# Step order in a fused attention and expert kernel: where the turn, the mix, the row-sum reciprocal and the gate's chain stand in four in-order queues

## The chip, the cores and the metric

The kernel runs on one core of one Trainium2 chip. The metric is the device time of one execution in microseconds, as the median over several executions. Five engines work side by side: PE (TensorE, matmuls and transposes), DVE (VectorE), ACT (ScalarE), POOL (GpSimd) and SP, which only issues transfers. Each takes its own instructions in the order in which the program wrote them.

## The reference, cut to what matters

```python
scores = scale * np.matmul(q, k.transpose(0, 1, 3, 2))        # 4 x 8 heads, 576 x 576, head_dim 64
kth = np.partition(scores, -32, axis=-1)[..., -32:-31]
scores = np.where(scores >= kth, scores, -1e9)
attn = np.exp(scores - np.max(scores, axis=-1, keepdims=True))
attn = attn / (np.sum(attn, axis=-1, keepdims=True) + 1e-09)
x = np.matmul(attn, v)                                        # -> 2304 tokens x 512
...
x = (x @ w_a) * (x @ w_b) @ w_out                             # 512 -> 1536 -> 512, gated
...
expert_idx = np.argmax(logits, axis=1)                        # logits of a cosine router, 8 experts
out[mask] = gate_w[mask, None] * (np.maximum(x[mask] @ w1[e], 0) @ w2[e])
```

Three stages follow one another: attention that keeps the 32 largest scores of each row, a gated feed-forward layer, and a layer of eight experts of which each token takes one.

## The kernel before, in words

**Rows and parts.** The attention is cut into 144 rows of work. A row is 128 query rows of one head pair against 576 keys. Four or five rows, in some stretches one, that share a pair of heads make a part of N = 256, 320 or 64 tokens; there are 36 parts. The main loop (line 919) runs over steps; in step s several rows are in flight, each at another stage. `scores` (359) of row s+2 is two halves of matmuls on PE, each followed by a copy to the tile `s` on ACT (372). `topk` (375) of row s is seven long passes on DVE, spread over two steps. `softmax` (399) of row s-2 is a Relu on ACT (404), then a small product and a subtraction on POOL (406, 407), and one step later an Exp on ACT (409) that also leaves the row sum in `sm`. `turn` (411) of row s-4 transposes the result on PE in two halves (426), each copied out by ACT (429). The tile `s` has five buffers (`SB`), so that the first copy of row s+2 needs the subtraction of row s-3.

**A part's end.** When the last row j of a part has been turned, in step j+4, `mix` (457) is put on a list, and its matmuls with the values (467) run in step j+5, followed by `along` (439), which turns the inverted row sums `rc` along the tokens with small matmuls (447) and copies them to `xR` on ACT (455). `sums` (432) adds 1e-9 on POOL at the start of step j+4 (435) and takes the reciprocal on DVE at the start of step j+5 (437), ahead of the long passes of that step. `finish` (477) multiplies by `xR` on POOL (479), splits the product into two parts and stores them; its pieces are taken one at a time in slots 2 and 4 of the following steps by `piece` (905).

**Background.** The gated layer, `moe1` (646), works on nine groups of 256 tokens. A group can start when its tokens have been finished, two steps later. It is a generator that hands out a few matmuls at a time (727 for the two first products, 674 for the second). `run` (884) carries out one slot of a step and then lets `background` (848) issue gated work worth `share[0]`. The share is set once a step (lines 992 to 1001): the allowance `STEP` = 5.4 (4.5 before step 38), less 0.54 for a turn, 0.48 or 0.96 for scores, 0.44 for turns of queries and keys, and N/100 as long as a mix is on the list, divided by the number of slots. A mix stays on the list for two steps: in the first it runs, in the second `run` finds it finished and takes it off, and no background is called for that slot.

**The gate's chain.** For each block f of a group ACT copies both products to `gab` (741), POOL multiplies them, ACT makes `gh`, POOL makes `gl` (all through line 661, `tick`, from the list `pend`); a tick comes after each four matmuls, seven to a block, and takes one entry of the list. Before, a block puts four entries on it: product, nothing, `gh`, `gl`.

**Order.** The order on PE, DVE, ACT and POOL is that of the program text (`manual_schedule`, 878). An instruction that waits holds all that stand behind it on its engine. Steps from `S1` = 19 on are called late; about 117 us have passed by then. After the last row the rest of the gated layer runs, then the experts.

Of the kernel before, what the change touches and what calls it, by code (L numbers as in the profile page):

```python
# [37 lines left out]
F0 = 1  # L38
# [47 lines left out]
def fused_kernel(  # L86
# [26 lines left out]
    NP = H // 2  # L113
# [91 lines left out]
    with ExitStack() as ph:  # L205
# [251 lines left out]
        def mix(o):  # L457
            N = o.N
            while pieces:
                piece()  # L460
            o.xsb = wk.tile([P, 320], F32, name="xsb")
            o.xh = wk.tile([P, 320], F32R, name="xh", bufs=1)
            p = ps.tile([P, 512], F32, name="tr", bufs=NTR)
            for c in range(5):
                ks = slice(0, P) if c < 4 else slice(64, P)
                for h in range(2):
                    pe.matmul(  # L467
                        p[h * 64 : h * 64 + 64, :N], o.vs[ks, h, c], o.wt[h][ks, c, :N], start=(c == 0), stop=(c == 4)
                    )
            act.activation(o.xsb[:, :N], p[:, :N], AF.Copy)  # L470
            along(o)
            pieces.append(finish(o))
            yield N / 100

        xg0 = [mk.tile([P, KC, GN], F32R, name=f"xg{i}", bufs=XG) for i in range(2)]

# [169 lines left out]
        def moe1(G):  # L646

            gi = G.gi
            g0, N = GROUPS[gi]
            G.inputs()  # L650
            xg, ws = G.xg, G.ws
            LA = WB // 2 - 1
            while len(ws) < LA:
                G.load()
            px = [None, None]
            gs = {}
            pend = []

            def tick():
                if pend:  # L660
                    pend.pop(0)[1]()  # L661

            def second(f, tiles=(0, 1)):
                while pend and pend[0][0] <= f:
                    tick()
                hi, lo = gs[f]
                if gi == 0:
                    conv.need(2, f)
                for t in tiles:
                    ts = slice(t * P, (t + 1) * P)  # L670
                    if f == 0:
                        px[t] = mp.tile([P, DM], F32, name="x1", bufs=2)
                    for i, (g, w) in enumerate(((lo, 0), (hi, 1), (hi, 0))):
                        pe.matmul(  # L674
                            px[t], g[:, ts], wo[:, w, f], start=(f == 0 and i == 0), stop=(f == NF - 1 and i == 2)
                        )
                    if f == NF - 1:
                        r = route(g0 // P + t, px[t])
                        next(r)
                        routes.append(r)  # L680
                        debt[1] = 0.0
                    tick()
                    yield 0.64

            begun = {}
            if gi == 0:
                for f in range(2):
                    while not (conv.ready(0, f) and conv.ready(1, f)):
                        yield None
                    begun[f] = [mp.tile([P, 512], F32, name=nm, bufs=2)[:, :256] for nm in ("ab", "x1")]  # L690
                    for i in range(2):
                        wt = conv.tiles[i, f]
                        for c in range(KC - 1):
                            for a, x in TERMS1:
                                pe.matmul(
                                    begun[f][i],
                                    wt[:, a, c, :],
                                    xg[x][:, c, :],
                                    start=(c == 0 and (a, x) == TERMS1[0]),
                                    stop=False,  # L700
                                )
                            yield 3 * N / 2400
                while ready[0] < N:
                    yield None

            for f in range(NF):
                nxt = todo[1][1] if len(todo) > 1 and todo[1][0] <= now[0] else None
                if f >= (NF - 4 if gi else NF - 1) and nxt:
                    nxt.inputs()
                if f + LA < NF:  # L710
                    G.load()
                elif nxt:
                    nxt.load()
                if gi == 0:
                    conv.begun = f
                    while now[0] < NRW and not (conv.ready(0, f) and conv.ready(1, f)):
                        yield None
                    for i in range(2):
                        conv.need(i, f)
                    ws[f] = [conv.tiles[i, f] for i in range(2)]  # L720
                ab = mk.tile([P, 2, GN], F32, name="gab")
                p = None if f in begun else mp.tile([P, 2, 256], F32, name="ab", bufs=2)
                ps_ = begun[f] if f in begun else [p[:, 0], p[:, 1]]
                for i, wt in enumerate(ws[f]):
                    terms = [(a, x, c) for (a, x) in TERMS1 for c in range(KC) if f not in begun or c == KC - 1]
                    for j, (a, x, c) in enumerate(terms):
                        pe.matmul(  # L727
                            ps_[i],
                            wt[:, a, c, :],
                            xg[x][:, c, :],  # L730
                            start=(j == 0 and f not in begun),
                            stop=(j == len(terms) - 1),
                        )
                        if j % 4 == 3 and (i == 0 or j < 11):
                            tick()
                            yield 4 * N / 2400
                if f in begun:
                    for i in range(2):
                        act.activation(ab[:, i], ps_[i], AF.Copy)
                else:  # L740
                    act.activation(ab, p, AF.Copy)  # L741
                recent[0] = ab
                yield 4 * N / 2400
                hi = mk.tile([P, GN], F32R, name="gh", bufs=LAG + 2)
                lo = mk.tile([P, GN], F32R, name="gl", bufs=LAG + 2)
                gs[f] = hi, lo
                pend.append((f, partial(pool.tensor_tensor, ab[:, 0], ab[:, 0], ab[:, 1], op=OP.mult)))
                pend.append((f, lambda: None))
                pend.append((f, partial(act.activation, hi, ab[:, 0], AF.Copy)))
                pend.append((f, partial(pool.tensor_tensor, lo, ab[:, 0], hi.bitcast(F32), op=OP.subtract)))  # L750
                if f >= LAG:
                    yield from second(f - LAG)
            tail[0] = tail[0] if gi == len(GROUPS) - 1 else lambda: None
            nxt = todo[1] if len(todo) > 1 and todo[1][0] <= now[0] and todo[1][1].ws else None
            if nxt:
                nxt[2] = moe1(nxt[1])
            for tiles in ((0,), (1,)) if gi == len(GROUPS) - 1 else ((0, 1),):
                for f in range(NF - LAG, NF):
                    for _ in range(6 if nxt else 0):
                        yield next(nxt[2])  # L760
                    for _ in range(NTF if tiles[0] >= ET else 0):
                        tail[0]()
                    yield from second(f, tiles)
# [155 lines left out]
        for step in range(-AHEAD_L, NRW + TL + 5):  # L919
# [24 lines left out]
            with tc.high_priority(offset=FG):  # L944
# [2 lines left out]
                    next(soft, None)  # L947
                soft, old = softmax(live[step - 2]) if 0 <= step - 2 < NRW else none, soft
                j = step - 5
                if 0 <= j < NRW and rows[j][4] and made[rows[j][:3]].n >= F0 * NP:  # L950
                    sums(made[rows[j][:3]], False)
                j = step - 3 if step < S1 else step - 4 if step > S1 else -1
                summed = made[rows[j][:3]] if 0 <= j < NRW and rows[j][4] else None
                if summed:
# [3 lines left out]
                for n in range(4):  # L958
                    next(thresholds[0], None)
                    next(cur, None)  # L960
                    if n == 3 and summed and summed.n < F0 * NP:
                        sums(summed, False)
                if step == NRW:
                    thresholds[0] = none
                elif 0 <= step < NRW:
                    thresholds[0] = cur
# [32 lines left out]
            if flips:  # L999
                cost, n = cost + 0.44, n + 2  # L1000
            share[0] = max((STEP0 if step < S0 else STEP) - cost, 0.0) / max(n, 1)
            for slot_, g in enumerate((tg, sg, tg, mg, sg)):
                if g is not none and not run(g) and g is mg and mixes:
                    mixes.pop(0)
                    mg = none
                with tc.high_priority(offset=FG):
                    if slot_ == 1:
                        next(soft, None)
                    elif slot_ == (2 if mg is not none else 3):
                        next(old if late else soft, None)  # L1010
                    elif slot_ == 4 and late:
                        next(soft, None)
# [414 lines left out]
```

## Time and profile before

| | |
|---|---|
| median of 3 executions | 1297.0 us (1294.22 to 1298.19) |
| the profiled execution | 1290.98 us, span 1289.2 us, mean granted TensorE clock 0.962 |
| PE, DVE busy | 1150.6 us, 918.7 us |
| ACT, POOL busy | 824.4 us, 726.7 us |

A row of a view with groups reads: line, engine, operation, output tile <- input tiles, shapes, count, then busy time in us and mean ns of one, then the engine's idle time just before them with what released it. A row of waits reads: the engine, tile and line that waited <- the one waited for, then us in total, times, and the longest in us. A row of stretches reads: from and to in us, the length, busy us with the number of instructions of each engine (PE, PEld, DVE, ACT, POOL, or of those that the line has), the granted clock as a share of full speed, the share of the DMA engines, GB/s. A row of the timeline reads: start, duration, engine, line, operation, and in brackets the idle time before it and its releaser.

### The profile page before, as it was taken

What the parts mean: (1) busy time and instruction counts of PE and PEld (TensorE: products, weight loads), DVE (VectorE), ACT (ScalarE), POOL (GpSimd) and SP (SyncE); (2) the same over time, 40 slices, a digit from 0 to 9 for tenths busy, and PEclk for the clock granted to TensorE, in tenths of its full rate; (3) what the DMA queues carried; (4) which work ended last, traced back from release to release, by engine and by line L of the source; (5) the groups of instructions that cost most, each with busy time, mean ns of one, the idle gap of its engine ahead of it and who ended that gap; (6) DMA issues with size and microseconds to landing.
All of it is one profiled execution on the core that took longest, in us unless ns stands there. A gap on an engine that the chain in (4) does not pass through costs nothing. (4 is left out here: it accounts for less than half of the span.)

```text
span 1289.2 us, 23924 instructions
## 1 busy us (share of the span) xinstructions
PE 1150.6 (89%) x8124; PEld 988.8 (77%) x8125; DVE 918.7 (71%) x2015; ACT 824.4 (64%) x1964; POOL 726.7 (56%) x1195
## 2 busy tenths in 40 slices
PE   5667997978998988999999899799999998999996
PEld 4445665767897876887887787687888877999995
DVE  8997998999897898899898899880210026565550
ACT  5776897877777777777777777673533225454541
POOL 5565786757676786767677767575445340223221
PEclk8788998989999997999999999899999999999999
DMA  7333676547684754765567566465987445556530
GB/s 232 115 127 125 220 226 237 199 153 219 197 261 154 194 182 133 225 191 180 175 196 222 181 188 195 135 198 182 346 249 227 158 129 184 189 171 208 200 115 27
DMA packets 129200, 240.05 MB, mean 186 GB/s; under 512 B 24896, under 2 KB 74176, under 8 KB 129074
## 3 DMA queue, kind: packets, MB, share of 16 engines
q1 hardware_dynamic: 125170, 228.74, 56.4%
q0 software_dynamic: 3904, 9.75, 2.0%
q8 instruction: 65, 1.06, 0.3%
q14 instruction: 61, 0.50, 0.1%
HBM read 198.38 MB, written 40.31 MB: 185 GB/s over the span
## 5 line engine op out<-in xcount | busy, mean ns | idle before, releaser
L392 DVE MAX8 t<-y 128x8 f32<-128x576 f32 x432 | 311.6, 749 | 2.7
L407 POOL TENSOR_TENSOR z<-s,z 128x576 f32<-128x576 f32 x144 | 205.7, 1429 | 70.5 <-ACT z L404 62.2
L395 DVE MATCH_REPLACE8 y<-t,y 128x576 f32<-128x576 f32 x288 | 213.9, 743 | 0.0
L727 PE MATMUL ab<-xg,wab 128*128 128x256 f32 x1398 | 206.0, 289 | 4.2 <-POOL xg L227 2.1
L426 PE MATMUL tr<-ident,z 128*128 128x128 f32 x720 | 135.9, 289 | 64.1 <-ACT z L409 62.1
L727 PEld LDWEIGHTS ab<-xg,wab 128*128 128x128 f32 x1398 | 182.4, 191 | 8.0 <-POOL xg L227 2.4
L727 PE MATMUL ab<-raw,wab 128*128 128x256 f32 x1152 | 172.8, 291 | 5.6 <-ACT gab L741 2.1
L372 ACT ACTIVATE s<-tr 128x288 f32<-128x288 f32 x288 | 118.5, 412 | 77.2 <-PE tr L371 39.2
L429 ACT ACTIVATE wt<-tr 128x384 f32<-128x384 f32 (+2 forms) x320 | 128.6, 415 | 48.6 <-PE tr L426 47.7
L727 PEld LDWEIGHTS ab<-raw,wab 128*128 128x128 f32 x1152 | 151.4, 192 | 9.3 <-ACT gab L741 2.7
L426 PEld LDWEIGHTS tr<-ident,z 128*128 128x128 f32 x720 | 90.1, 146 | 85.6 <-ACT z L409 77.1
L661 POOL TENSOR_TENSOR gab<-gab 128x256 f32<-128x256 f32 x108 | 81.7, 757 | 108.0 <-ACT gab L741 97.5
L674 PE MATMUL x<-wo,gh 128*128 128x512 f32 x432 | 134.8, 393 | 0.0
L371 PE MATMUL tr<-kT,qT 128*128 128x288 f32 x512 | 127.2, 334 | 3.0 <-ACT qT L348 1.8
L1081 DVE TENSOR_TENSOR u<-raw,u 128x1024 fp32r<-128x1024 f32 x64 | 75.9, 1221 | 73.6 <-ACT u L1080 55.3
L1134 POOL DMA_INDIRECT out_dram<-o,ids x24 | 31.5, 1313 | 170.8 <-ACT o L1133 120.9
L392 DVE MAX8 t<-s 128x8 f32<-128x576 f32 x144 | 107.1, 744 | 12.5 <-ACT s L372 12.4
L661 POOL TENSOR_TENSOR gl<-gab,gh 128x256 fp32r<-128x256 f32 x108 | 81.4, 754 | 59.8 <-ACT gh L661 44.1
L409 ACT ACTIVATE z<-z,bi 128x576 f32<-128x576 f32 x144 | 112.2, 779 | 0.3 <-POOL z L407 0.3
L404 ACT ACTIVATE z<-s,bi 128x576 f32<-128x576 f32 x144 | 111.6, 775 | 0.2 <-DVE bi L397 0.2
L395 DVE MATCH_REPLACE8 y<-t,s 128x576 f32<-128x576 f32 x144 | 106.9, 742 | 0.0
L467 PE MATMUL tr<-wt,vs 128*64 128x256 f32 (+5 forms) x720 | 97.9, 411 | 1.3 <-ACT kT L332 1.3
(201 smaller groups left out, 2238.2 us busy)
## 6 DMA issues: line engine op xcount, KB each, us to landing
wab<-wab_d SPq DMA_DIRECT2D x192, 512.0 KB, 4.6
raw<-in_moe_w_dram SPq DMA_DIRECT2D x28, 1024.0 KB, 5.5
wab_d<-wab SPq DMA_DIRECT2D x24, 512.0 KB, 3.3
kT<-kT_d SPq DMA_DIRECT2D x20, 576.0 KB, 4.9
vs<-in_v_dram SPq DMA_DIRECT2D x36, 256.0 KB, 3.1
kT_d<-kT SPq DMA_DIRECT2D x16, 576.0 KB, 5.2
raw<-in_moe_w_a_dram SPq DMA_DIRECT2D x12, 512.0 KB, 4.2
raw<-in_moe_w_b_dram SPq DMA_DIRECT2D x12, 512.0 KB, 4.9
```

The source lines that it names most:

```text
L371: pe.matmul(p, l, r, start=(i == 0), stop=(i == len(terms) - 1))
L372: act.activation(t.s[:, cs], p, AF.Copy, scale=SCALE)
L392: dve.max(v, cur)
L395: dve.match_replace(out=rest, in_to_replace=v, in_values=cur, imm_value=LOWEST)
L404: act.activation(t.w, t.s, AF.Relu, bias=t.bi[:, 1:2], scale=-HUGE)
L407: pool.tensor_tensor(t.w, t.s, t.w, op=OP.subtract)
L409: act.activation(t.w, t.w, AF.Exp, bias=t.bi[:, 0:1], accum_out=t.o.sm[:, t.slot : t.slot + 1])
L426: pe.transpose(pt[:, i * P : (i + 1) * P], t.w[:, k0 : k0 + P], ident)
L429: act.activation(th[:, sl, w], pv[:, :, src], AF.Copy)
L661: pend.pop(0)[1]()
L674: pe.matmul(px[t], g[:, ts], wo[:, w, f], start=(f == 0 and i == 0), stop=(f == NF - 1 and i == 2))
L727: pe.matmul(ps_[i], wt[:, a, c, :], xg[x][:, c, :], start=(j == 0 and f not in begun), stop=(j == len(terms) - 1),)
```

## The change

In `mix` the point at which the generator stops moves ahead of `along`: the first call runs the matmuls with the values, the second, a step later (or at the next part's end, if that is sooner), runs `along` and puts `finish` on the list. After the first call the charge for the second step is 40/100 and not N/100. In late steps the five slots go scores, turn, mix, turn, scores, where they went turn, scores, turn, mix, scores; the Exp of the row before is issued in slot 2 in all late steps, where it was slot 2 with a mix on the list and slot 3 without one. The reciprocal comes after the long DVE passes of step j+5 and not ahead of them. In the gate's chain an empty entry stands ahead of the product and another ahead of `gl`.

```diff
@@ mix
             act.activation(o.xsb[:, :N], p[:, :N], AF.Copy)
+            yield N / 100
             along(o)
             pieces.append(finish(o))
-            yield N / 100
@@ moe1
+                pend.append((f, lambda: None))
                 pend.append((f, partial(pool.tensor_tensor, ab[:, 0], ab[:, 0], ab[:, 1], op=OP.mult)))
                 pend.append((f, lambda: None))
                 pend.append((f, partial(act.activation, hi, ab[:, 0], AF.Copy)))
+                pend.append((f, lambda: None))
                 pend.append((f, partial(pool.tensor_tensor, lo, ab[:, 0], hi.bitcast(F32), op=OP.subtract)))
@@ the main loop
                 j = step - 5
-                if 0 <= j < NRW and rows[j][4] and made[rows[j][:3]].n >= F0 * NP:
-                    sums(made[rows[j][:3]], False)
+                inverted = made[rows[j][:3]] if 0 <= j < NRW and rows[j][4] else None
...
                     if n == 3 and summed and summed.n < F0 * NP:
                         sums(summed, False)
+                    if n == 3 and inverted and inverted.n >= F0 * NP:
+                        sums(inverted, False)
...
-            for slot_, g in enumerate((tg, sg, tg, mg, sg)):
+            for slot_, g in enumerate((sg, tg, mg, tg, sg) if late else (tg, sg, tg, mg, sg)):
                 if g is not none and not run(g) and g is mg and mixes:
                     mixes.pop(0)
                     mg = none
+                elif g is mg:
+                    parts_n[0] = 40
                 with tc.high_priority(offset=FG):
                     if slot_ == 1:
                         next(soft, None)
-                    elif slot_ == (2 if mg is not none else 3):
+                    elif slot_ == (2 if late or mg is not none else 3):
                         next(old if late else soft, None)
                     elif slot_ == 4 and late:
                         next(soft, None)
```

## Rows read from the trace of the kernel before

**Rows 1.** The page: busy time of the engines over the span.

```profile
PE 1150.6 (89%) x8124; PEld 988.8 (77%) x8125; DVE 918.7 (71%) x2015; ACT 824.4 (64%) x1964; POOL 726.7 (56%) x1195
```

**Rows 2.** Busy time by stretch, all engines: the late steps, and the rest after them.

```profile
150.00:865.00 715.00, 648.43 (x4784) 545.70 (x4782) 647.30 (x1471) 540.04 (x1372) 500.90 (x840) 0.97 0.63 193
...
865.00:1050.00 185.00, 175.52 (x1230) 158.31 (x1230) 23.93 (x77) 71.87 (x187) 86.74 (x193) 0.99 0.66 210
```

**Rows 3.** What PE waited for, 150 to 865 us.

```profile
PE tr L426 <- ACT z L409: 31.5, 32, 3.2
...
PE ab L727 <- ACT gab L741: 3.4, 5, 0.7
```

**Rows 4.** What DVE waited for, 150 to 865 us.

```profile
DVE rc L437 <- POOL rc L435: 40.3, 18, 7.2
DVE t L392 <- ACT s L372: 11.7, 11, 2.7
```

**Rows 5.** The page's groups of the softmax and of the gate's chain.

```profile
L407 POOL TENSOR_TENSOR z<-s,z 128x576 f32<-128x576 f32 x144 | 205.7, 1429 | 70.5 <-ACT z L404 62.2
...
L661 POOL TENSOR_TENSOR gab<-gab 128x256 f32<-128x256 f32 x108 | 81.7, 757 | 108.0 <-ACT gab L741 97.5
...
L661 POOL TENSOR_TENSOR gl<-gab,gh 128x256 fp32r<-128x256 f32 x108 | 81.4, 754 | 59.8 <-ACT gh L661 44.1
...
L404 ACT ACTIVATE z<-s,bi 128x576 f32<-128x576 f32 x144 | 111.6, 775 | 0.2 <-DVE bi L397 0.2
```

**Rows 6.** Busy time of line 727 alone in three successive steps (PE, PEld).

```profile
630.40:636.80 6.40, 0.48 (x4) 0.56 (x4) 1.00 0.57 175
636.80:640.07 3.27, 0.16 (x2) 0.00 (x0) 1.00 0.51 140
640.07:646.36 6.29, 3.99 (x28) 3.58 (x28) 1.00 0.61 184
```

**Rows 7.** Timeline of PE right after the second of these steps.

```profile
640.07 0.55 PE L426 MATMUL tr<-ident,z 128*128 128x128 f32 x3 [1.03 <-ACT z L409]
...
641.40 0.43 PE L371 MATMUL tr<-kT,qT 128*128 128x288 f32 x2
```

**Rows 8.** Timeline of ACT around the second of these steps.

```profile
632.96 0.41 ACT L372 ACTIVATE s<-tr 128x288 f32<-128x288 f32 x1 [1.52 <-POOL z L407]
...
639.15 0.77 ACT L409 ACTIVATE z<-z,bi 128x576 f32<-128x576 f32 x1
```

**Rows 9.** Busy time of line 727 alone in two stretches without background work.

```profile
481.00:499.00 18.00, 0.00 (x0) 0.00 (x0) 0.81 0.36 109
814.10:823.50 9.40, 0.00 (x0) 0.07 (x1) 0.96 0.54 180
```

**Rows 10.** What ACT and POOL waited for, 150 to 865 us.

```profile
ACT s L372 <- POOL z L407: 29.3, 23, 2.8
POOL xsb L479 <- ACT xR L455: 22.3, 14, 2.7
```

**Rows 11.** Groups of a part's end, whole span.

```profile
L479 POOL TENSOR_TENSOR xsb<-xsb,xR 128x256 f32<-128x256 f32 (+2 forms) x36 | 26.7, 742 | 28.2 <-ACT xR L455 28.1
...
L447 PE MATMUL tr<-ident,rc 128*64 128x128 f32 (+1 forms) x320 | 25.9, 276 | 0.0
...
L437 DVE RECIPROCAL rc<-rc 128x4 f32<-128x4 f32 (+2 forms) x36 | 6.3, 176 | 48.3 <-POOL rc L435 48.3
```

**Rows 12.** What PE waited for, 485 to 865 us.

```profile
PE ab L727 <- DMA raw<-xl_d: 1.7, 1, 1.7
```

**Rows 13.** Busy time by stretch, all engines: two of seven stretches at half clock.

```profile
491.61:498.43 6.82, 5.48 (x26) 5.03 (x25) 6.79 (x17) 5.43 (x13) 5.51 (x9) 0.50 0.36 103
...
822.70:829.53 6.83, 6.58 (x31) 5.29 (x33) 6.80 (x17) 3.95 (x11) 2.23 (x3) 0.50 0.01 2
sum 40.96, PE 36.07 PEld 27.28 DVE 38.90 ACT 27.04 POOL 22.65; mean PE 5.15 PEld 3.90 DVE 5.56 ACT 3.86 POOL 3.24
```

## The prediction

> **What bounds the kernel now.** I read the busy times first [rows 1], then the same by stretch [rows 2]. The change acts from about 117 us to the end of the attention rows. In the 715 us from 150 to 865 us PE is busy for 648 and DVE for 647: neither is full, each stands still for about 67 us. After 865 us DVE has almost nothing to do, PE is busy for 175.5 of 185 us with the gated layer that is left over, and the experts follow. The matmuls are the same before and after, so what counts is PE's idle time: a microsecond of it that goes brings the end nearer, whichever step the background work is done in. DVE's idle time counts only where DVE holds something up.
>
> The waits say which of the two leads. Nearly half of PE's 67 us is one wait: the first transpose of a turn for the Exp of the same row, 31.5 us in 32 times [rows 3]. DVE's largest is the reciprocal for POOL's addition, 40.3 us in 18 times [rows 4]. But the Relu on ACT, the first user of DVE's thresholds, waited 0.2 us for them in the whole span [rows 5]: DVE is ahead. Its stops at the reciprocal only eat up that lead.
>
> Why PE waits is seen in three successive steps [rows 6]. The first, 6.40 us, holds a mix. In the second, 3.27 us, line 727 has 0.16 us on PE, the end of the work before: the mix is still on the list and is charged for, though it has run. The third begins with a wait of 1.03 us for an Exp [rows 7] that ACT had started at 639.15; ACT itself had lost 1.52 us in the first step, when the copy of the scores waited for POOL's subtraction [rows 8]. PE rushes through the empty step and stands before the turn; ACT can't follow.
>
> **The change part by part.**
>
> *The charge for the second step.* A mix is on the list in two steps for 29 parts (36, less the four early ones that finish at once and three one-row parts). In the second, with turn and scores and no queries to turn, four slots call for background. Before: (5.4 - 0.54 - 0.48 - 3.2) / 5 = 0.24 a slot, 0.94 us; for N = 256 it is 1.46. After: (5.4 - 1.42) / 5 = 0.80 a slot, 3.18 us. So these steps get about 2.0 us more, 58 us over 29 parts. It is moved from later, not new: its own gain is nothing, but it lies between the Exp and the turn that waits for it.
>
> *`along` a step later.* The small matmuls are 25.9 / 36 = 0.72 us a part [rows 11] in both cases; they too move from the full step to the empty one.
>
> *Slots.* The turn now comes after a scores half, 0.43 us on PE [rows 7], and its share of background. Exp is issued earlier in steps without a mix, and behind the mix's copy in steps with one, where a mix, a half turn, a half of scores and the slots' shares cover it.
>
> For a turn that follows a second step, cover grows by 0.43 + 0.72 + 2.0 = 3.1 us, above the mean wait of 31.5 / 32 = 0.98. But in two stretches, 18 and 9.4 us, there is no background at all [rows 9], for the next group's tokens aren't ready; there the cover grows by 0.43 alone. I estimate six of the waits there, one of them the longest: 3.2 + 5 x 0.98 = 8.1 us, of which 6 x 0.43 = 2.6 goes. The other 31.5 - 8.1 = 23.4 goes whole. Together **-26 us**; bounds 0 and -31.5.
>
> *The multiplication in `finish`.* It was taken in slot 4, after the subtraction had been issued; now slot 2 puts it ahead of that step's subtraction on POOL, waiting for `xR`. It waited 22.3 us in 14 times before [rows 10], 1.6 each, and takes 0.74 [rows 11]. What it holds is the subtraction, then the copy of scores and the Exp on ACT. The cover of 3.1 us is above 1.6 + 0.74, so I take 0.15 us a part, **+4 us**; bounds nothing, and 29 times the mean of today's waits of that copy, 29.3 / 23 = 1.27 [rows 10], 37 us.
>
> *Moving the copy of the scores ahead.* In slot 0 it meets the same subtraction one half turn earlier. ACT will wait more often, before a copy of a turn that PE hasn't made yet; I take nothing, its bound is in the 37 us.
>
> *The gate's chain.* POOL lost 108.0 us before 108 products and 59.8 us before as many `gl` [rows 5]. Standing one tick and two ticks later, both hold up POOL's queue less, and the subtraction behind them comes earlier; I count this as cover, not as gain. At a group's last block the list isn't empty when the second product wants `gl`: it is then issued right ahead of PE's wait. At 0.75 us and the mean idle of 0.55 before it, eight groups cost at most 10 us; attention work stands in between while rows run, so **+2 us**.
>
> *The reciprocal.* 0.18 us each [rows 11], now behind seven passes. POOL's addition is done by then, so most of the 40.3 us goes. It goes to the copies of scores, for which DVE waited 11.7 us [rows 4], and into a longer lead: **0**. The lead hides it. Were it gone, each DVE microsecond would come through, and the bound is 647 busy of 715: DVE leaves room for 67 us. `along` reads the reciprocal a step later, with DVE ahead: no wait.
>
> *Group starts.* `finish` stores its two halves half a step later, some 3 us, on SP's queue; nothing else on it changes order. PE waited 1.7 us once for such a load [rows 12]. More background a step means that a group ends sooner and the next isn't ready: the empty stretches grow, their steps are quick, and the load is waited for. Five starts at 0 to 3 us: **+3 us**.
>
> *The clock.* Between 150 and 865 us the granted clock is 0.50 in seven stretches, 41.0 us together, with PE busy for 36.1 of them [rows 13], at 1.2 and not 2.4 GHz: some 18 us lost. Two of them fall into or right after the empty stretches [rows 9, 13]. Fewer waits favour the high level, longer empty stretches the low one; I take 0, with 9 us either way. The Trainium skill ("TensorE: Matmul & The Clock Gate", "HAM oscillation") says that pauses of PE send its clock back to the low level and that the matmuls behind the pause then start there; by that rule the filled steps would give back more than their waits, and the sum would be -35 and not -17. The trace agrees as far as that falls stand at the empty stretches; that it would pay here no row shows.
>
> Sum: -26 + 4 + 2 + 3 = **-17 us**. The profiled execution took 1290.98 us around its span of 1289.2; it becomes 1274. It lies 6.0 us under the median of 1297.0, so the median goes to **1280**.
>
> **The rivals.**
>
> *A. Forecast:* the waits at the turn go, small new ones come: 1280, its own range 1266 to 1291. Chance 0.60.
>
> *B. The clock comes along.* Without the rush and the stop at each part's end PE stays at 2.4 GHz in most of the 41 us: another -18, 1262. For it: falls at 491 and 822 us stand by empty stretches; against it: those stay. Chance 0.12.
>
> *C. Readiness binds.* Each group's work must lie between its tokens' readiness and the next's. Work done earlier only makes the empty stretch longer; there the pace is set by DVE, whose 647 us equal PE's 648, and the 26 us come back as waits for thresholds or for Exp: 1297. For it: background already runs dry twice [rows 9]. Against it: DVE's lead, lengthened by up to 40.3 us of stops that go. Chance 0.14.
>
> *D. Slower: the subtraction.* The multiplication that waits for `xR` ahead of it, and the scores' copy moved to slot 0, make ACT wait for POOL in every second step of a mix. It decides once the subtraction ends more than the cover of 3.1 us late. At its upper bound it costs 37 us, and with the other terms, -26 + 2 + 3, the sum is +16: 1313. For it: 23 such waits already [rows 10]; against it: 1.6 + 0.74 is below 3.1. Chance 0.14.
>
> **How the numbers follow.** A change of 0.3%, 3.9 us, is about what a measurement of this kernel can tell from none. A and B are faster, 0.72 (A's own upper end is 1291); C is no change, 0.14; D is slower, 0.14. The low end takes the bounds of the first term and of the clock, -31.5 - 9 + 4, about 1260; the high end reaches through C to 1299 and leaves out D and the tail of B, 2 in 10.
>
> **What would show it.** In the profile after: PE's wait at line 426 for line 409 under 10 us where 31.5 stood; line 727 with 2 to 3 us on PE in the step behind each mix; DVE's wait at the reciprocal under 8 us and its wait for scores grown; POOL's idle time before the gate's product down. PE's idle time from 150 us to the end of the gated layer should fall by about as much as the span. Wrong would be: a wait of ACT's copy of scores for POOL well above 29 us, with PE idle as long as before (D); Relu waiting for DVE, and empty stretches of more than 30 us (C); or half-clock stretches that change by more than 20 us either way.

## The result, and the profile after

The changed kernel takes 1308.27 us (median of 6 runs, 1302.84 to 1315.5), the kernel before on the same chip 1294.53: a ratio of 1.0111 [1.0074, 1.0148], so 1.1% slower. Forecast were 1280 us and a range up to 1299. The profiled execution took 1308.08 us around a span of 1306.3, 17.1 us more than before.

The page after, busy times, granted clock in 40 slices, and three groups:

```profile
PE 1174.9 (90%) x8124; PEld 1003.8 (77%) x8125; DVE 920.8 (70%) x2015; ACT 820.7 (63%) x1964; POOL 727.1 (56%) x1195
...
PEclk8787998969999997999999899899999999999999
...
L426 PE MATMUL tr<-ident,z 128*128 128x128 f32 x720 | 138.8, 297 | 37.2 <-ACT z L409 35.0
...
L404 ACT ACTIVATE z<-s,bi 128x576 f32<-128x576 f32 x144 | 112.0, 778 | 0.8 <-DVE bi L397 0.8
...
L661 POOL TENSOR_TENSOR gab<-gab 128x256 f32<-128x256 f32 x108 | 82.5, 764 | 62.4 <-ACT gab L741 46.9
```

The first line is the one to start with [rows 1]: 8124 matmuls as before, but PE is busy for 1174.9 us where it was 1150.6. Since span = PE busy + PE idle, the +17.1 us are +24.3 of busy time and only -7.2 of idle (138.6 to 131.4). The count of matmuls is the same, so I looked at the clock. Added up from the trace's clock records, the time at half clock after the first 120 us (without the last fall, at the end of the program) went from 47.8 to 95.6 us; the mean granted clock fell from 0.962 to 0.946. Over the whole span PE was busy at half clock for 76.4 us before and 115.9 after. Half of the difference, 19.8 us, is an estimate of what the clock has in the +24.3.

What PE waited for, 150 to 865 us (one line per wait):

```profile
PE tr L371 <- ACT qT L348: 9.1, 7, 1.8
PE tr L371 <- ACT wt L429: 7.5, 9, 1.6
PE tr L426 <- ACT z L409: 6.8, 7, 1.3
PE x L674 <- POOL gl L661: 6.6, 5, 2.5
PE tr L314 <- ACT s L372: 5.3, 5, 2.9
...
PE ab L727 <- DMA xg<-xl_d: 4.1, 2, 3.2
```

The wait for the Exp went from 31.5 us [rows 3] to 6.8. But five others stand beside it now, 32.6 us together; over all waits in this stretch PE's sum went from 66.2 to 56.2 only. The first two are new places for the same stop: in the new order the scores (371) come right behind the turns of queries (348) and the turn's copies (429), and wait for them 16.6 us, where 1.5 stood. The step behind a mix has changed as well. The busy time of line 727 alone, in the step of a mix, the next and the one after:

```profile
620.12:626.04 5.92, 1.92 (x12) 1.64 (x12) 1.00 0.68 209
626.04:632.28 6.24, 4.58 (x30) 3.75 (x28) 1.00 0.45 128
632.28:638.50 6.22, 3.74 (x26) 3.15 (x24) 1.00 0.80 232
```

The step behind a mix is no longer empty: 4.58 us of line 727 where 0.16 stood [rows 6], and it takes 6.24 us, not 3.27. That this isn't what removed the wait for the Exp is shown by e2 and e5 below.

The other engines' waits in the same stretch, DVE, ACT and POOL in turn:

```profile
DVE t L392 <- ACT s L372: 61.9, 37, 5.7
...
DVE rc L437 <- POOL rc L435: 4.3, 2, 2.4
```

```profile
ACT s L372 <- POOL z L407: 48.3, 40, 3.8
```

```profile
POOL xsb L479 <- ACT xR L455: 80.4, 20, 6.9
POOL gab L661 <- ACT gab L741: 21.9, 18, 5.4
```

DVE's stop at the reciprocal moved to its wait for scores, as said [rows 4]. POOL now stands 80.4 us at the multiplication by `xR`, up to 6.9 at a time, where it stood 22.3 [rows 10], and ACT's copy of scores waits 48.3 us for the subtraction behind it.

Where the clock went is seen in the stretches without background. First line 727 alone, then all engines, after; then all engines in the two such stretches of before [rows 9]:

```profile
478.50:512.00 33.50, 0.00 (x0) 0.00 (x0) 0.76 0.34 110
704.00:727.00 23.00, 0.00 (x0) 0.00 (x0) 0.85 0.36 111
820.00:849.00 29.00, 0.00 (x0) 0.00 (x0) 0.82 0.30 97
```

```profile
478.50:512.00 33.50, 24.46 (x145) 18.65 (x143) 30.36 (x68) 28.46 (x74) 25.37 (x41) 0.76 0.34 110
704.00:727.00 23.00, 17.09 (x104) 12.21 (x104) 19.17 (x42) 18.96 (x51) 16.38 (x29) 0.85 0.36 111
820.00:849.00 29.00, 20.21 (x122) 12.72 (x120) 22.50 (x52) 20.27 (x50) 18.34 (x38) 0.82 0.30 97
sum 85.50, PE 61.76 PEld 43.58 DVE 72.03 ACT 67.69 POOL 60.09; mean PE 20.59 PEld 14.53 DVE 24.01 ACT 22.56 POOL 20.03
```

```profile
481.00:499.00 18.00, 13.92 (x92) 10.51 (x90) 16.53 (x37) 15.41 (x39) 14.83 (x28) 0.81 0.36 109
814.10:823.50 9.40, 3.80 (x28) 3.06 (x27) 6.44 (x16) 7.54 (x19) 7.78 (x24) 0.96 0.54 180
sum 27.40, PE 17.72 PEld 13.57 DVE 22.97 ACT 22.95 POOL 22.61; mean PE 8.86 PEld 6.79 DVE 11.49 ACT 11.47 POOL 11.31
```

They grew from 27.4 to 85.5 us, with a new one at 704. PE stands still in them for 85.5 - 61.8 = 23.7 us (before 9.7), and the clock column says that 33 us of them are at half clock (twice one less the clock, times the length: 16.1 + 6.9 + 10.4; before 7.6). The three are the longest, and other stretches count too: before has three of 11 to 15 us earlier on, after one of 16. Over all stretches of more than 5 us without matmuls of the gated layer, from 120 us to the last turn, the length goes from 98.7 to 158.0 us and the half clock in them from 35.1 to 65.6, but PE's idle time only from 27.9 to 32.8. What sets the pace of most of their steps is on DVE: all engines in the larger part of the first one, and DVE's timeline there, its last operation of each row:

```profile
484.00:512.00 28.00, 20.93 (x123) 15.56 (x122) 27.86 (x62) 23.70 (x62) 20.40 (x29) 0.74 0.38 122
```

```profile
490.92 0.14 DVE L397 TENSOR_SCALAR bi<-t 128x1 f32<-128x1 f32 x1
496.00 0.14 DVE L397 TENSOR_SCALAR bi<-t 128x1 f32<-128x1 f32 x1
501.08 0.14 DVE L397 TENSOR_SCALAR bi<-t 128x1 f32<-128x1 f32 x1
506.17 0.14 DVE L397 TENSOR_SCALAR bi<-t 128x1 f32<-128x1 f32 x1
```

DVE is busy for 27.86 of 28 us, a row every 5.08 us. In the other two stretches a row takes as long behind two longer steps each (7.8 and 6.3 us, 9.7 and 7.1). With nothing to fill PE, such a step is as long as DVE needs, and PE's spare time is lost. At half clock (1.2 GHz, the level that these rows show) PE stays behind the stretch's end too:

```profile
263.50:284.00 20.50, 17.88 (x78) 12.96 (x77) 19.19 (x43) 12.30 (x30) 12.26 (x18) 0.50 0.34 107
505.90:519.60 13.70, 11.41 (x52) 8.61 (x52) 13.63 (x33) 7.49 (x18) 8.77 (x13) 0.50 0.45 136
```

The first goes 8 us beyond an empty stretch that ends at 276 us, the second 7.6 us beyond the first one shown. The second half of the last turn starts at 901.1 us (before 880.8), the gated layer ends at 1047.1 (before 1031.6).

### The profile page after: what moved, and what is told of

Its sections match the earlier page's. It is cut to its first block, busy times and chain, and to the rows that moved or that the text cites. A ratio compares the mean times of both kernels' runs of the same rounds, so it can differ in the third digit from the quotient of the medians.

```text
span 1306.3 us, 23925 instructions
## 1 busy us (share of the span) xinstructions
PE 1174.9 (90%) x8124; PEld 1003.8 (77%) x8125; DVE 920.8 (70%) x2015; ACT 820.7 (63%) x1964; POOL 727.1 (56%) x1195
## 5 line engine op out<-in xcount | busy, mean ns | idle before, releaser
L426 PE MATMUL tr<-ident,z 128*128 128x128 f32 x720 | 138.8, 297 | 37.2 <-ACT z L409 35.0
L372 ACT ACTIVATE s<-tr 128x288 f32<-128x288 f32 x288 | 118.5, 415 | 84.5 <-POOL z L407 48.3
L371 PE MATMUL tr<-kT,qT 128*128 128x288 f32 x512 | 131.3, 342 | 18.4 <-ACT qT L348 9.4
L661 POOL TENSOR_TENSOR gab<-gab 128x256 f32<-128x256 f32 x108 | 82.5, 764 | 62.4 <-ACT gab L741 46.9
L371 PEld LDWEIGHTS tr<-kT,qT 128*128 128x128 f32 x512 | 89.2, 208 | 30.7 <-ACT qT L348 12.8
L467 PE MATMUL tr<-wt,vs 128*64 128x256 f32 (+5 forms) x720 | 102.5, 426 | 0.0
```

Source lines behind the costliest of these rows:

```text
L371: pe.matmul(p, l, r, start=(i == 0), stop=(i == len(terms) - 1))
L372: act.activation(t.s[:, cs], p, AF.Copy, scale=SCALE)
L426: pe.transpose(pt[:, i * P : (i + 1) * P], t.w[:, k0 : k0 + P], ident)
L467: pe.matmul(p[h * 64 : h * 64 + 64, :N], o.vs[ks, h, c], o.wt[h][ks, c, :N], start=(c == 0), stop=(c == 4))
```

## The experiments

Theory T (Theory 1 in the first expectations): the background is handed out faster than groups become ready; the empty stretches grow, PE idles there at DVE's pace and falls to half clock. Rival R (Theory 2): the slots and the late `along` hold up POOL's subtraction and the queue of pieces, so that copies and loads come late. All ratios are against the kernel before on the same chip, with 95% intervals. Half clock is counted after the first 120 us and without the last fall, idle is span less busy; both, and the span, are of one execution.

| run | ratio | span | PE busy | PE idle | half clock |
|---|---|---|---|---|---|
| before | 1 | 1289.2 | 1150.6 | 138.6 | 47.8 |
| after | 1.0111 [1.0074, 1.0148] | 1306.3 | 1174.9 | 131.4 | 95.6 |
| e1 charge back | 1.0116 [1.0092, 1.0139] | 1300.9 | 1162.8 | 138.1 | 75.1 |
| e2 charge alone | 1.0020 [0.9999, 1.0042] | 1292.2 | 1165.2 | 127.0 | 92.2 |
| e3 pieces later | 1.0279 [1.0262, 1.0296] | 1321.8 | 1174.5 | 147.3 | 109.2 |
| e4 STEP 4.9 | 0.9951 [0.9934, 0.9967] | 1278.6 | 1153.4 | 125.2 | 61.4 |
| e5 slots alone | 1.0327 [1.0304, 1.0349] | 1320.1 | 1165.4 | 154.7 | 81.9 |
| e6 gate alone | 0.9942 [0.9924, 0.9960] | 1274.4 | 1144.8 | 129.6 | 47.8 |
| e7 reciprocal alone | 1.0014 [0.9992, 1.0035] | 1285.6 | 1149.4 | 136.2 | 54.6 |
| e8 e7 + late along | 1.0115 [1.0093, 1.0138] | 1302.5 | 1166.9 | 135.6 | 78.5 |
| e9 e5, six buffers | 1.0082 [1.0054, 1.0110] | 1292.1 | 1152.0 | 140.1 | 64.9 |
| e10 as after | 1.0152 [1.0123, 1.0182] | 1305.3 | 1175.9 | 129.4 | 105.8 |
| e11 after, old slots | 1.0146 [1.0112, 1.0180] | 1306.3 | 1164.8 | 141.5 | 92.2 |
| e12 before + gate, charge, STEP 5.0 | 0.9797 [0.9764, 0.9829] | 1263.2 | 1141.1 | 122.1 | 47.8 |
| e13 e8 + third place | 0.9992 [0.9968, 1.0015] | 1294.5 | 1163.7 | 130.8 | 75.1 |
| e14 after, old along | 1.0125 [1.0092, 1.0159] | 1305.0 | 1164.3 | 140.7 | 92.2 |
| e15 after, filled | 1.0094 [1.0062, 1.0126] | 1300.1 | 1176.3 | 123.8 | 51.2 |
| e16 before + gate, STEP 5.0 | 0.9831 [0.9798, 0.9863] | 1265.9 | 1135.2 | 130.7 | 34.1 |
| e17 after + third place | 1.0078 [1.0051, 1.0105] | 1302.0 | 1173.9 | 128.1 | 95.6 |
| e18 after, six buffers | 1.0110 [1.0074, 1.0146] | 1297.1 | 1168.2 | 128.9 | 88.7 |

**The charge and the pace (e1, e2, e4).**

```diff
@@ e1, from after (e2 puts the same two lines into before)
-                elif g is mg:
-                    parts_n[0] = 40
@@ e4, from after
-STEP = 5.4
+STEP = 4.9
```

> The changed kernel with the old charge of N/100 in the step behind a mix; all else as changed. Theory 1 (the lower charge hands out the background too early, the empty stretches grow from 21 and 9 us to 35, 24 and 31 us and the clock falls in them): empty stretches and half-clock time go back towards those of before (about 48 us after 120 us, where the changed kernel has 92), the waits at the turn stay under 12 us, 1283 us or less, faster than before. Theory 2 (the multiplication of finish ahead of the subtraction on POOL, and the copy of the scores in slot 0, hold up ACT): 1300 to 1310 us, POOL still waits over 70 us for xR.

> The kernel before with the lower charge alone (40/100 in the step behind a mix). Theory 1: empty stretches as in the changed kernel, half-clock time above 80 us, 8 to 15 us slower than before, though the wait of the turn for the Exp falls by half or more. Theory 2: the wait of the turn for the Exp goes and nothing takes its place, 10 to 25 us faster than before.

> The changed kernel with the allowance STEP at 4.9 and not 5.4, which takes back about as much background over all steps as the lower charge adds in 29 of them (58 us over 122 steps, 0.5 each). Theory 1: empty stretches shrink below 25 us, half-clock time falls to 50 us or less, 1280 to 1288 us, faster than before. Theory 2: no gain, 1303 to 1313 us.

The charge alone (e2) shows half of T. Idle falls by 11.6 us, busy time grows by 14.6, and the empty stretches are 36, 24 and 26 us long: nothing is gained (1.002), but the loss of 8 to 15 us that T expected isn't there. And the wait for the Exp, which both theories expected to fall, stays (120 to 900 us; before 34.8 us in 36 times):

```profile
PE tr L426 <- ACT z L409: 33.6, 26, 2.7
```

So filling the step behind a mix doesn't remove that wait. Taken back out of the changed kernel (e1), the charge shortens the empty stretches to 20 and 17 us and busy time by 12, but idle time rises by 6.7, ACT's copy waits 71.9 us for the subtraction, POOL 77.3 for `xR`, and the time stays (1.0116), as R expected. So something else costs there. With less handed out per step (e4) the empty stretches after 120 us are 19, 15 and 17 us, busy time is back to 1153.4, idle falls too, and the kernel is below the one before, as T expected (half clock at 61.4 us and not 50):

```profile
PE 1153.4 (90%) x8124; PEld 990.7 (77%) x8125; DVE 918.5 (72%) x2015; ACT 814.1 (64%) x1964; POOL 725.1 (57%) x1195
```

This is the largest gain that a single edit brought the changed kernel, and it changes nothing but the pace. It doesn't show that the lower charge was the cause, though: without that charge a smaller allowance gains 1.1% as well (e6 to e16, 0.9942 to 0.9831).

**The parts alone (e5, e6, e7, e8), and each part with its cause removed (e9, e13).**

```diff
@@ e5, from before (and Exp in slot 2 of late steps)
-            for slot_, g in enumerate((tg, sg, tg, mg, sg)):
+            for slot_, g in enumerate((sg, tg, mg, tg, sg) if late else (tg, sg, tg, mg, sg)):
@@ e9, from e5
-ZB = 4
+ZB = 3
-SB = 5
+SB = 6
@@ e6, from before: the two empty entries in the gate's chain
@@ e7, from before: the reciprocal behind the passes
@@ e8, from e7: the yield of mix ahead of along
@@ e13, from e8
-                if slot_ in (2, 4):
+                if slot_ in (2, 4) or slot_ == 1 and late:
                     piece()
```

> The kernel before with the new order of slots in late steps alone (scores, turn, mix, turn, scores; Exp in slot 2). Theory 1 (the charge is what cost): the cover of the turn grows, its wait for the Exp falls below 15 us of 33, 5 to 15 us faster than before. Theory 2 (order on POOL and ACT is what cost): ACT's wait for the subtraction rises from 29 us, same or up to 10 us slower.

> The slots alone, as in the run that was 3.3% slower, but with six score buffers and not five (and three buffers for z and not four, for the room), so that the first copy of scores in a step needs the subtraction of the row before the one it needed. Theory 3 (the copy in slot 0 stands too close behind the subtraction that frees its buffer): ACT's wait at the copy of scores for the subtraction falls from 104 us below 25 us and most of the 40 us loss goes, 1285 to 1300 us. Rival (the loss is the scores that meet queries just turned, PE at line 371 for lines 348 and 429, 26 us, which no buffer changes): still 1318 us or more.

> The kernel before with the two empty entries in the gate's chain alone. Theory 1 and 2 alike: POOL's idle time before the gate's product falls from 108 us towards 65 us, PE waits up to 8 us more for gl at a group's end; within 5 us of before. A change of more than that means that the gate's place in POOL's queue matters more than either theory has it.

> The kernel before with the reciprocal behind the long passes alone. Theory 1: DVE's wait at the reciprocal falls from 48 us below 12 us and its wait for scores rises by as much; within 4 us of before, since DVE is ahead. Theory 2: the same DVE waits, but along may stand still for the reciprocal in the same step: up to 10 us slower.

> The kernel before with the late reciprocal and with along a step behind the mix, but the old charge and the old slots. Theory 1: the step behind the mix holds 0.7 us more on PE, within 5 us of before. Theory 2: the multiplication of finish now comes right behind the along that it waits for, in the same slot 4; POOL's wait for xR rises from 28 us to 60 us or more and 8 to 15 us are lost.

> The late along with the late reciprocal alone (1.0115 of before), with a third place for the list of pieces in late steps (slot 1). If the late along costs because the list of finish and of the splitting of keys runs late: PE's wait for the split keys falls from 19 us below 8 us and most of the loss goes, 1285 to 1296 us, ratio 0.995 to 1.004. Rival (the loss is the late row itself: the copy to xR and POOL's product sit in another place): 1.009 or more.

The slots alone cost 3.3%, far more than either theory gave them. What PE and ACT waited for in e5, 120 to 900 us:

```profile
PE tr L371 <- ACT qT L348: 14.5, 8, 2.4
PE tr L371 <- ACT wt L429: 11.4, 13, 1.2
...
PE tr L426 <- ACT z L409: 3.2, 5, 1.3
```

```profile
ACT s L372 <- POOL z L407: 104.2, 65, 4.6
```

Here the wait for the Exp is gone (3.2 us, before 34.8) with the old charge: it is the order of the slots, with the place of the Exp, that takes it away. The time doesn't follow. Line 371 now waits 25.9 us, and PE's idle time is 16.1 us longer than before. ACT's wait was 29.3 us in 23 times before. Slot 0 puts the first copy of scores half a turn nearer to the subtraction that frees its buffer. A sixth buffer `s`, at the price of one buffer `z`, removes this wait from ACT's list and takes back three quarters of the loss (1.0082); the waits at line 371 stay, 22.0 us. So this cost, which the prediction put at nothing inside a bound of 37 us, is real.

The late `along` costs 1.0% over e7, though not by POOL's wait for `xR`, which Theory 2 expected at 60 us or more (3.3). What PE waited for in e8, and below in e13, 120 to 900 us:

```profile
PE tr L314 <- POOL ks L227: 19.1, 4, 8.7
PE tr L426 <- ACT z L409: 17.9, 17, 2.8
```

```profile
PE tr L314 <- POOL ks L227: 9.4, 4, 6.0
```

`ks` is the split of the next part's keys, and it stands in the same list of pieces as `finish` (473, 981), which is emptied in two places a step. A `finish` that enters a step later pushes it back, and the next part's first transposes wait for it. A third place for pieces takes the loss back wholly (0.9992). The third place and the sixth buffer were not run in the kernel before by themselves, so a gain of their own isn't excluded.

The gate's entries gain 0.6%, where the prediction had +2 us and both theories nothing above 5 us; the reciprocal changes nothing, as forecast.

**What of this holds the changed kernel (e3, e11, e14, e17, e18).**

```diff
@@ e3, from after
+                had = bool(pieces)
                 if g is not none and not run(g) and g is mg and mixes:
...
-                if slot_ in (2, 4):
+                if slot_ == 4 or slot_ == 2 and had:
@@ e11, from after: slots and Exp as in before
@@ e14, from after: the yield of mix behind along, as in before
@@ e17, from after: third place for pieces, as in e13
@@ e18, from after: six buffers, as in e9
```

> The changed kernel, but the first piece of finish, the multiplication, is not taken in the slot in which along is issued; it comes in slot 4 behind the subtraction. Theory 1: within 5 us of the changed kernel, since the background is handed out as before. Theory 2: POOL's wait for xR falls from 87 to under 40 us, ACT's wait for the subtraction from 48 to about 29 us, and 10 to 20 us are gained, 1290 to 1298 us.

> The changed kernel with the old order of slots and the old place of the Exp; the late along, the lower charge, the late reciprocal and the gate's empty entries stay. If the slots cost in company what they cost alone (3.3%): 1265 to 1280 us, faster than before. If along and the mix hide the slots' cost, so that what is left comes from the late along (1.0% alone): 1295 to 1310 us.

> The changed kernel with along again in the step of the mix; the slots, the late reciprocal, the lower charge and the gate's entries stay. If the late along is what the changed kernel loses by: 1278 to 1290 us, ratio 0.985 to 1.000. Rival (with the old mix the slots cost what they cost alone, as the late along had taken load from the step of the mix): 1310 us or more, ratio above 1.015.

> The changed kernel with a third place for the list of pieces in late steps (slot 1). If the late list holds the changed kernel (q, k and the groups' inputs come late): 1285 to 1297 us, ratio 0.995 to 1.004. If the copy of the scores behind the subtraction holds it: within 5 us of the changed kernel, ratio 1.008 or more.

> The changed kernel with six score buffers (and three for z). If the copy of the scores behind the subtraction holds it: ACT's wait at the copy falls from 48 us below 15 us and 10 us or more are gained, ratio 1.003 or less. If the late list holds it: ratio 1.007 or more, though that wait goes.

No part of R, taken out by itself, brings the time back. Old slots leave 1.0146, the old `along` 1.0125, six buffers 1.0110 (ACT's wait goes and the loss stays), the third place 1.0078. With old slots the wait for the Exp is back (32.5 us) and those for `ks` and `qs` grow to 12.4 and 9.1; with the old `along` ACT's wait for the subtraction grows to 67.1. Both taken out at once, at the same pace, were not run, so R as a whole isn't refuted: charge, gate and reciprocal alone would leave about 0.998 if their ratios multiply (an estimate from e2, e6 and e7). Old slots and the old `along` each lower busy time by 10 us and raise idle by as much; in e14 the empty stretches are longer still, 42, 26 and 33 us. e3 delays `finish`, meant to free the subtraction, and makes all worse, where neither theory had a loss: POOL's wait for `xR` goes (2.1 us), but the waits for `ks` and `qs` grow to 12.8 and 9.8 us, and one empty stretch is 41 us long.

**Is it the clock itself (e10, e15)?**

```diff
@@ e10, from after, in background
+            if 38 <= now[0] < NRW and not routes and not (todo and todo[0][0] <= now[0]):
+                pt = mp.tile([P, 512], F32, name="ab", bufs=2)
+                for _ in range(4):
+                    pe.matmul(pt[:, :256], identr, wo[:, 0, 0, :256], start=True, stop=True)
@@ e15, from after, in scores
+                if 38 <= now[0] and not (todo and todo[0][0] <= now[0]):
+                    terms = [(x, o.kT[:, 0, cs]) for x in (identr, minusr, identr, minusr)] + terms
```

> The changed kernel, with four matmuls of 256 columns without use on PE at each call for background that finds no group ready and no routing under way (steps 38 to 143). Clock theory (PE's busy time grew by 24 us since the clock falls in the longer empty stretches, and that is the loss): half-clock time after 120 us falls from 96 to 65 us or less, and although useless work is added the time falls by 5 to 15 us, 1293 to 1303 us. Rival (the clock only shows that the rows move slowly for another reason): the added work costs what it takes, 1308 us or more.

> The changed kernel, with four more matmuls of 288 columns in each half of the scores (identity and minus identity on the keys, which add up to nothing) in steps from 38 on in which no group is ready; about 1 us of PE a step at full clock. If the clock's falls are a cause: half-clock time after 120 us falls from 96 to 70 us or less and, with some 20 us of added work, the time stays within 5 us of the changed kernel or falls. If they are a sign only: half-clock time may fall, but the time grows by 10 us or more.

In e10 the matmuls that nobody reads were left out of the program (8124 on PE), so it tests neither side and is a second measurement of the changed kernel: 1.0152 beside 1.0111. In e15 they are there. The first engine line of its page, and the added matmuls by form:

```profile
PE 1176.3 (90%) x8284; PEld 1011.7 (78%) x8285; DVE 927.5 (71%) x2015; ACT 819.9 (63%) x1964; POOL 726.7 (56%) x1195
```

```profile
L373 PE MATMUL tr<-kT,identr 128*128 128x288 f32 x80 | 26.8, 348 | 4.6 <-ACT wt L431 4.6
...
L373 PE MATMUL tr<-kT,minusr 128*128 128x288 f32 x80 | 23.5, 308 | 0.0
```

The two groups overlap. With each moment counted once the added matmuls take 32.5 us of PE, in stretches without gated work, and the rest of the work takes 1157.4 us, 17.5 less than in the changed kernel. Half clock fell to 51.2 us; the time is level with the changed kernel's or a little below it (1.0094). By the words of the expectation this is the side on which the clock is a cause, but a clock that was won back and work that was added could also have cancelled out. The 28 us shown above for the changed kernel, now in e15, tell more:

```profile
484.00:512.00 28.00, 23.17 (x165) 18.51 (x165) 27.86 (x64) 20.36 (x52) 18.18 (x26) 0.91 0.37 115
```

The clock is 0.91 where it was 0.74, PE holds more work, and DVE is busy for the same 27.86 us. The four longest empty stretches are 16, 35, 24 and 33 us long, in the changed kernel 16, 35, 24 and 31. Two things follow. The empty stretches do send the clock down, since filling them keeps it up. And within most of their length neither PE's clock nor PE's load sets the time: DVE does, at 5.08 us a row, in this run as well. With nearly the half clock of the kernel before (51.2 beside 47.8) e15 is still 0.9% slower than it. The 24.3 us of busy time are therefore partly a sign of PE's lost room and not all of them a cost by itself.

**The edits that help, put together (e12, e16).** Both start from before; e12 has the gate's entries, the lower charge and `STEP` = 5.0, e16 the same without the charge.

> The kernel before with the gate's empty entries and the lower charge, and the allowance STEP at 5.0. Theory 1 (the filled step saves PE's idle time, 12 us with the charge alone, and what it costs is the clock in longer empty stretches, 15 us): with less background a step the clock cost goes and the saving stays, on top of the gate's 8: 1268 to 1276 us, 1.3% or more faster than before. Rival (the charge is of no use): 1278 us or more.

> The kernel before with the gate's empty entries and STEP at 5.0, without the lower charge. If the lower charge carries the gain once the background lasts (theory 1): 1276 to 1284 us, ratio 0.988 to 0.996, that is 10 us or more behind the kernel with the charge (0.980). Rival (the smaller allowance alone does it): 1262 to 1270 us.

```profile
PE 1141.1 (90%) x8124; PEld 987.1 (78%) x8125; DVE 919.1 (73%) x2015; ACT 822.1 (65%) x1964; POOL 728.0 (58%) x1195
```

e12 takes 1265.46 us, 0.9797 [0.9764, 0.9829], and beats both kernels; e16 0.9831 [0.9798, 0.9863]. Their intervals overlap, so what the charge adds isn't shown; e16 itself came out as the rival said (1268.74 us). In e16 the empty stretches after 300 us are at most 9 us and the wait for the Exp 38.2 us, more than before, and yet it is 1.7% faster: that wait was not what the kernel lost its time to. Nor do long stretches decide alone: e12, the fastest, has three of 22, 22 and 17 us, with the half clock of before. e4, with the same charge and gate, nearly the same pace (4.9 beside 5.0), and the slots, the late `along` and the reciprocal besides, stands at 0.9951 on another chip: about 1.5% is what those cost at this pace, more than the 1.1% of the whole change.

## Why the prediction was wrong

**What held, and what held by luck.** The wait for the Exp fell by 24.7 us, forecast -26, but not for the reason given. Two of the 3.1 us of cover were to come from the filled step behind a mix. That step is filled (4.58 us on line 727, where 2 to 3 were expected), yet with the charge alone the wait stays at 33.6 us, and with the slots alone it falls to 3.2. The size was right by luck. The reciprocal held: 40.3 to 4.3 us, and nothing in the time. The gate's product waits less on POOL, 108.0 to 62.4 us [rows 5]; that this gains 0.6% instead of costing 2 us was missed.

**The first step that failed** is "the other 23.4 goes whole": that a microsecond of PE's waiting which goes brings the end nearer. While this one wait fell by 24.7 us, PE's waits together fell by 10.0 (66.2 to 56.2), since 15.1 came back at line 371 alone. In e5 the same wait is gone, PE's idle time is 16.1 us longer and the time 3.3%; in e16 it is longer than before and the time 1.7% shorter. Over the whole span PE's idle time fell by 7.2 us, where the sum had 17.

**The second** is the pair "Group starts" (+3) and "The clock" (0, 9 us either way). It measured +24.3 us of busy time. The prediction said that the empty stretches would grow, and priced only the load at a group's start. That load did cost (3.23 us in front of one group):

```profile
611.88 1.19 PE L727 MATMUL ab<-xg,wab 128*128 128x256 f32 x4 [3.23 <-DMA xg<-xl_d]
```

But the stretches grew by 58 us, and in most of them DVE sets the step. PE was busy at half clock in all stretches of more than 5 us for 30.2 us before and 56.6 after; half of the difference, 13.2 us, and the 4.9 us of idle time that were added there make some 18 us of PE's room lost in them (an estimate). That is rival C's mechanism, with its sign in the profile as named (a stretch above 30 us), except that Relu hardly waited for DVE (0.8 us, where [rows 5] had 0.2). What reaches PE there are mostly waits for ACT's copies and the Exp; by which links DVE's pace comes to them was not followed further. C's price was also added up wrongly: if "the 26 us come back", the other terms, +4 + 2 + 3, are left, and the sum is 1306 and not 1297. B had the sign wrong: the clock came along, but downward, +47.8 us of half clock where a change by over 20 was named as a refutation. The Trainium skill's rule on pauses of PE ("TensorE: Matmul & The Clock Gate", "HAM oscillation") is that they send its clock back to the low level. The trace agrees: 65.6 of the 95.6 us of half clock stand in the stretches of more than 5 us, and e15, which fills them, has 51.2. The prediction worked out only what the filled steps would give by it, and left the longer pauses inside its 9 us.

**The terms of the subtraction** (+4, and nothing for the copy) were too small as well: ACT's wait for it went from 29.3 to 48.3 us, POOL's for `xR` from 22.3 to 80.4, and the slots alone cost 3.3%, some 40 us, above the bound of 37. Rival D names this place and ends near the measured time (1313). In the changed kernel this wait doesn't decide by itself: PE's idle time fell, and neither a sixth buffer nor old slots bring the time back.

**What stays open.** The parts don't add up: alone 1.033, 1.010, 1.001, 1.002 and 0.994, together 1.011. The charge, with its longer stretches, gains nothing (e2), and the slots and the late `along` together cost about 1.5% at the smaller allowance (e4 beside e12). Whether they are the whole loss at 5.4 is not shown, as the run without both is missing. Six buffers `s` beside four of `z` were not tried, there being no room for both.

## What to carry to other kernels

Split a change of the span into busy and idle time of the engine that leads: more busy time at an equal count of matmuls points to the clock, and asks where PE ran out of work. Where a background fills an engine, the pace at which it is handed out has to match the pace at which its inputs become ready; filling a gap here empties a stretch there, and in it the next engine sets the time. Before a wait is priced as gain, ask where it will turn up again: here it went and the time grew (e5), and a kernel with more of it was faster (e16). When several edits are to remove one wait, try each alone (e2, e5); a piece that is moved later also delays what shares its list (e8, e13).

## What was not expected

Added matmuls that take 32.5 us of PE in the empty stretches left the time where it was or lowered it (1.0094 beside 1.0111 and 1.0152), with half clock down from 95.6 to 51.2 us. Matmuls whose result nobody reads were not executed at all (e10). The same program as the changed kernel gave 1.0111 and 1.0152 at two times, 0.4% apart, so differences between kernels measured at different times are read no finer than that.
